# Laying out a kernel's instruction order with PSUM accesses of two engines in sequence, measured prices, a preference for long-ready TensorE groups, and shared buffers

## The chip, the cores and the metric

The kernel runs on one core of one Trainium2 chip. Time is the device time of one execution in microseconds (us). TensorE is PE in the profile, its weight loads PEld, VectorE DVE, ScalarE ACT, GpSimd POOL, SyncE SP.

## The reference

Sliding-window attention (window 64) feeds a feed-forward block whose activation is a rational function:

```python
def _attn_ref(q, k, v):                 # 8 x 8 heads x 576 x 64
    scores = scale * np.matmul(q, k.transpose(0, 1, 3, 2))
    rel = pos[:, None] - pos[None, :]
    scores = np.where((rel >= 0) & (rel < 64), scores, -1000000000.0)
    attn = np.exp(scores - np.max(scores, axis=-1, keepdims=True))
    attn = attn / (np.sum(attn, axis=-1, keepdims=True) + 1e-09)
    return np.matmul(attn, v)

def _moe_ref(x, w_in, w_out, a, b):     # x: 4608 x 512, w_in: 512 x 2048, w_out: 2048 x 512
    h = x @ w_in
    P = a[0] + a[1] * h + a[2] * h * h + a[3] * h * h * h
    Q = 1.0 + np.abs(b[0]) * np.abs(h) + np.abs(b[1]) * h * h
    return (P / (Q + 1e-06)) @ w_out
```

x is the attention's output with its heads side by side. All inputs are float32.

## The kernel before, in words

The 4608 tokens are cut into 12 chunks of 384 (`CH`). The width of 2048 is cut into 16 slices of 128. One step is one chunk with one slice: 192 steps. The phases run chunk 0 and then chunk 1 over the first eight slices, chunk 1 and then chunk 0 over the last eight, and then chunks 2 to 11 over all sixteen.

**A step.** `ffn1` makes h (128 slice rows x 384 tokens) in one of two PSUM banks (`h_ring`). Each float32 factor is held as a high and a low part, and three of the four products are taken, so h takes 12 matmuls (4 pieces of 128 x 3 terms) and the second layer 9 (3 blocks of 128 tokens x 3 terms). The gate follows: ACT reads h three times (Square into u, Abs into r, Identity into num), DVE makes Q from u and r, ACT takes Ln and Exp of it (1/Q), DVE makes P in num with two more reads of h, then the high part gh, two operations on u and the low part gl. `ffn2`, three steps later (`LAG`), multiplies gl and gh with the weights into the PSUM banks `ps_o` (o).

**An attention unit** is one chunk with one pair of heads, 48 in all: q, k and v are loaded, the scores go to `ps_s` (`score_products`), the mask is added on PE in chunks 0 to 2 and on DVE later, DVE takes the maximum, ACT makes six exponentials with sums (`unit_soft`), DVE normalises (`unit_norm`; "sm<-sm,rs"), PE transposes six blocks into `ps_s` (`unit_transpose`), ACT copies them to pT, PE multiplies by v into `ps_x` (`value_products`), and ACT and DVE split the result into xh and xl. A unit of chunk c runs beside the steps of the chunk before.

**Weights.** The 32 weight tiles (16 of w_in, 16 of w_out) are fetched into six spare places and three slots (`w_ring`, w_st), rebuilt by ACT and DVE into c (w_c) and split into high (ACT) and low (DVE) parts (`load_weight`). The next fetch of a slot is recorded behind the tile that it frees.

**The order.** Nothing is issued where it is written. A `Planner` records every operation with the engine, the bytes that it reads and writes and a price (`cost`: the time for which it occupies the engine, and the time to its result). `plan` then lays the operations out engine by engine: the one with the earliest possible start goes next, and among those ready on that engine the one recorded first. `emit` issues them in the order of the planned starts, and each engine then works through its instructions in that order, waiting where the framework's semaphores say so. All recorded instructions carry line 226, so the profile is read by tiles. `group` makes several matmuls one entry of the plan; `fill` puts warm-up matmuls in early gaps.

**Buffers.** r, u and num have two places each (`tmp`), gh and gl four each, sm and q/k two each, pT one, c two.

Of the kernel before, what the change touches and what calls it, by code (L numbers as in the profile page):

```python
# [9 lines left out]
F32 = mybir.dt.float32  # L10
# [11 lines left out]
CH = 384  # L22
# [3 lines left out]
LAG = 3  # L26
GB = 4
SLOTS = 3
WARM = 7
FILL = 430  # L30
C1AT = 0, 0, 1, 3
ON_PE = 2
# [18 lines left out]
class Planner:  # L51
# [4 lines left out]

    def __init__(self, nc, free, shares):
        self.nc, self.shares = nc, shares
        self.ops, self.group_op = [], None
        self.free = dict(free)  # L60
# [49 lines left out]
    def cost(self, engine, method, out, reads, kw, args):  # L110
        if isinstance(out, Late):
            n = out.size // 4
        else:
            n = 1
            for _, k in out.ap[1:]:
                n *= k
        if engine == "SP":
            parts = 128 if isinstance(out, Late) else (out.ap[0][1] if out.tensor.__class__.__name__ != "DRamTensorHandle" else 0)
            size = mybir.dt.size(out.dtype) * n * (parts or out.ap[0][1])
            return 400, 400, size  # L120
        if engine == "PE":
            if method == "transpose":
                return 109, 270, 0
            if isinstance(args[2], Late):
                n = args[2].size // 4
            else:
                n = 1
                for _, k in args[2].ap[1:]:
                    n *= k
                if args[2].dtype == F32:  # L130
                    return (45, 270, 0) if args[1].ap[0][1] == 64 else (52, 225, 0)
            return n * 0.452, n * 0.452 + 165, 0
        if engine == "ACT":
            if "accum_out" in kw:
                return 343, 450, 0
            f = args[2] if len(args) > 2 else None
            occ = 58 + 0.813 * n
            if n == 512:
                occ = 640 if method == "copy" and getattr(out, "dtype", None) == F16 else 510
            for k in ("scale", "bias"):  # L140
                if isinstance(kw.get(k), bass.AP):
                    occ += 92
            if f in (AF.Ln, AF.Exp):
                occ += 55
            return occ, occ + 120, 0
        if engine == "DVE":
            if method == "tensor_reduce":
                n = 1
                for _, k in reads[0].ap[1:]:
                    n *= k  # L150
            if n < 16:
                return 90, 185, 0
            occ = 65 + 1.045 * n
            if isinstance(kw.get("scalar"), bass.AP):
                occ += 62
            return occ, occ + 85, 0
        if engine == "POOL":
            return (n * 2.0 + 60, n * 2.0 + 100, 0) if method in ("tensor_scalar", "tensor_copy") else (n * 2.4 + 130, n * 2.4 + 170, 0)

    def add(self, op):  # L160
        op.index, op.before, op.after = len(self.ops), set(), []
        op.ready = max([self.known.get(name, 0) for name, *_ in op.reads + op.writes], default=0)
        for is_write, spans in ((False, op.reads), (True, op.writes)):
            for name, p0, p1, b0, b1 in spans:
                for q0, q1, c0, c1, other, wrote in self.hist.get(name, ()):
                    if (wrote or is_write) and p0 < q1 and q0 < p1 and b0 < c1 and c0 < b1:
                        op.before.add(other)
# [6 lines left out]
        for wrote, spans in ((False, op.reads), (True, op.writes)):  # L174
            for name, p0, p1, b0, b1 in spans:
                h = self.hist.setdefault(name, [])
                if wrote:
                    h[:] = [x for x in h if not (p0 <= x[0] and x[1] <= p1 and b0 <= x[2] and x[3] <= b1)]
                h.append((p0, p1, b0, b1, op.index, wrote))
                if name in self.shares:  # L180
                    self.hist.setdefault(self.shares[name], []).append((0, 128, 0, 1 << 20, op.index, False))

    def plan(self):
# [6 lines left out]
        for _ in self.ops:  # L190
            start, engine = min((max(self.free[e], min(o.ready for o in w)), e) for e, w in waiting.items() if w)
            op = min((o for o in waiting[engine] if o.ready <= start), key=lambda o: o.index)
            waiting[engine].remove(op)
# [35 lines left out]
class Recorder:  # L229
# [3 lines left out]
    def __getattr__(self, method):  # L233
        return lambda *args, **kw: self.planner.record(self.engine, self.owner, method, args, kw)


# [11 lines left out]
def swa_rational_ffn(ctx: ExitStack, tc: tile.TileContext, qk, v, w_in, w_out, out):  # L248
# [56 lines left out]

    warm = const.tile([P, 512], BF16, name="warm")
    nc.vector.memset(warm, 0.0)
    for _ in range(WARM):
        nc.tensor.matmul(ps_o[2], warm[:, 0:P], warm, start=True, stop=True)
    make_mask()  # L310
# [28 lines left out]
    UNIT = QKAB + TC * P  # L339
    qk_ring = Ring(ring, 2, [P, QKAB], F32, "qk")  # L340
    vt_ring = Ring(ring, 2, [P, TC * P], F32, "vt")
    w_ring = Ring(ring, SLOTS, [P, 1026], F32, "w_st")
    spare = [late.tile([P, H * NCC * P], F32, name=f"early_{n}", tag=f"late_{n}") for n in ("wi_h", "wi_l")]
    spare_slots = [t[:, k * 1026:(k + 1) * 1026] for k in range(H * NCC * P // 1026) for t in spare]
    c_ring = Ring(ring, 2, [P, 512], F32, "w_c")
    top_ring = Ring(const, 0, [], F32, "top")
    top_ring.tiles = tops
    sm_ring = Ring(ring, 2, [P, 2, PR, P], F32, "sm")
    pT_ring = Ring(ring, 1, [P, 2, PR * P], F32, "pT")
    small = {n: Ring(ring, 2, [P, 2 * PR], F32, n) for n in ("nmx", "sums", "rs")}  # L350
    tmp = {n: Ring(ring, 2, [P, CH], F32, n) for n in ("r", "u", "num")}
    g_ring = [Ring(ring, GB, [P, CH], F32R, n) for n in ("gh", "gl")]
    ob_ring = Ring(ring, 2, [P, DO], F32, "ob")

    shares = {t.tensor.name: f"late_{n}" for t, n in zip(early + spare, ("wo_l", "wo_h", "wi_h", "wi_l"))}
    pl = Planner(nc, dict(DVE=4700, ACT=2100, PE=WARM * 430 + 1200, POOL=5000, SP=750), shares)
    pl.ready_at(mask, 4300)
# [12 lines left out]
    def load_weight(which, i):  # L370
        w = staged.pop((which, i))
        f = (lambda t: t.rearrange("p c n -> p (c n)")) if which == "in" else (lambda t: t)
        hi_name, lo_name = ("wi_h", "wi_l") if which == "in" else ("wo_h", "wo_l")
        top, c = top_ring(), c_ring()
        low = w.bitcast(U32)[:, 0:1024].rearrange("p (n two) -> p n two", two=2)[:, :, 1]
# [13 lines left out]
    def load_qk(c, hp):  # L389
        qk_t = early[hp // 2][:, hp % 2 * UNIT:hp % 2 * UNIT + QKAB] if c == 0 else qk_ring()  # L390
        pl.sync.dma_start(out=qk_t, in_=qk[hp, c])
# [48 lines left out]
    def score_maximum(c, hp):  # L440
        u = live[c, hp]
        on_pe, ps, both, m = u["on_pe"], u["ps"], u["both"], u["m"]
        sm, nmx = u["sm"], u["nmx"] = sm_ring(), small["nmx"]().rearrange("p (z r) -> p z r", z=2)
        if not on_pe:
# [30 lines left out]
    def unit_transpose(c, hp):  # L475
        u = live[c, hp]
        ps, both = two_banks(c, hp, True)
        with pl.group():
            for j in range(2 * PR):
                pl.tensor.transpose(ps[j // PR][:, (j % PR) * P:(j % PR + 1) * P], u["sm"][:, j, :], ident)  # L480
        pT = u["pT"] = pT_ring()
        if both is not None:
# [33 lines left out]

    def ffn1(c, i):
        h = h_ring()[:, 0:CH]
        n = 0
# [9 lines left out]
        r, u, num = (tmp[n]() for n in ("r", "u", "num"))  # L529
        gh, gl = (g() for g in g_ring)  # L530
        pl.scalar.activation(u, h, AF.Square)
        pl.scalar.activation(r, h, AF.Abs, scale=b_raw[:, 0:1])
        pl.scalar.activation(num, h, AF.Identity, scale=a_sb[:, 3:4], bias=a_sb[:, 2:3])
# [9 lines left out]
        gs[c, i] = gh, gl  # L543
# [4 lines left out]
    part = {}  # L548

    def ffn2(s):  # L550
# [89 lines left out]
    for s in range(total + LAG):  # L640
# [3 lines left out]
        if s < total:  # L644
            ffn1(*steps[s])
        for fn, *args in todo.get(s, ()):
# [4 lines left out]
    pl.plan()  # L651
    pl.fill("PE", ps_o[2].tensor.name, FILL, (nc.tensor.matmul, (ps_o[2], warm[:, 0:P], warm), dict(start=True, stop=True)))
    pl.emit()
# [37 lines left out]
```

## Time and profile before

| | |
|---|---|
| median of 3 runs | 982.18 us (982.14 to 982.31) |
| the profiled execution | 982.07 us, of which the span in the profile is 980.3 |
| mean granted TensorE clock | 0.997 |
| busy: PE, DVE, ACT | 952.6 (97%), 911.2 (93%), 698.5 us (71%) |
| bytes by DMA | 68.38 MB, mean 70 GB/s |

The rows of the trace are read thus. A timeline row is start, duration, engine, line, operation and output<-inputs, then a count and, in brackets, the idle time of the engine before it and what ended that. A row of the waits is engine and output, what it waited for, total us, number of times and the longest. Bars of successive matmuls overlap, since a matmul starts before the one ahead of it has drained; the spacing of their starts is what they cost. A stage row has the window, its length, and busy time with instruction counts for PE, PEld, DVE, ACT and POOL, then the granted clock, the DMA share and GB/s.

### The profile page before, as it was taken

Reading aid. Unit: us, or ns where it says so; the run is one execution under the profiler, and the core shown is the slowest. Engines: PE = TensorE matmul, PEld = TensorE weight load, DVE = VectorE, ACT = ScalarE, POOL = GpSimd, SP = SyncE. Lnnn points to the kernel's source line nnn. Section 1 sums busy time; section 2 is a strip of 40 time slices with the busy share of each in tenths; the row PEclk is TensorE's granted clock in tenths of the full one; section 3 lists DMA queues with packets and bytes.
Section 4 is the critical chain, followed back from the end, with each engine's and each line's share of the span. In section 5 each row is a group of like instructions: output and inputs, shape, how many; then the busy total and the mean of one; then the engine's idle time right before and its main releaser. Section 6 shows DMA issues by size and latency. Waiting matters only on the chain.

```text
span 980.3 us, 17701 instructions
## 1 busy us (share of the span) xinstructions
PE 952.6 (97%) x6672; PEld 824.6 (84%) x6675; DVE 911.2 (93%) x1747; ACT 698.5 (71%) x1737; POOL 4.4 (0%) x20
## 2 busy tenths in 40 slices
PE   8899999999999999999999999999999999999998
PEld 5677788888888888888888888888888888888996
DVE  6999999998999999999999999999999899999996
ACT  7988777776667667767677677667766776676664
POOL 1000000000000000000000000000000000000000
PEclk9999999999999999999999999999999999999999
DMA  9344341313103103103102200210310310300000
GB/s 360 127 171 147 122 150 39 96 50 117 51 1 117 35 17 118 35 17 116 37 17 74 79 17 26 93 51 1 118 35 17 118 35 18 100 1 2 33 1 32
DMA packets 24564, 68.38 MB, mean 70 GB/s; under 512 B 2720, under 2 KB 2720, under 8 KB 24480
## 3 DMA queue, kind: packets, MB, share of 16 engines
q1 hardware_dynamic: 24480, 67.27, 20.2%
q8 instruction: 52, 0.85, 0.4%
q14 instruction: 32, 0.26, 0.1%
HBM read 57.03 MB, written 10.22 MB: 69 GB/s over the span
## 4 chain that ended last, share of the span: by engine, by line
PE 64%; DVE 19%; ACT 10%; issue 2%; DMA 1%; ACTq 0%; DVEq 0%
PE o L226 29%; PE h L226 28%; DVE u L226 6%; PE ps_s L226 5%; ACT sm L226 4%; DVE num L226 3%; PE ps_x L226 3%; ACT r L226 2%; DVE gh L226 2%; DVE sm L226 2%; DVE nmx L226 1%; ACT u L226 1%; DVE gl L226 1%; DMA w_st<-w_out 1%; ACT num L226 1%
## 5 line engine op out<-in xcount | busy, mean ns | idle before, releaser
L226 PE MATMUL h<-xl,wi_h 128*128 128x384 f32 x768 | 260.4, 339 | 7.7 <-DVE num L226 6.2
L226 PE MATMUL h<-xh,wi_l 128*128 128x384 f32 x768 | 258.1, 336 | 0.0
L226 PE MATMUL h<-xh,wi_h 128*128 128x384 f32 x768 | 257.9, 336 | 0.0
L226 PE MATMUL o<-wo_h,gl 128*128 128x512 f32 x576 | 236.5, 411 | 2.5 <-DVE gl L226 1.7
L226 PE MATMUL o<-wo_h,gh 128*128 128x512 f32 x576 | 228.2, 396 | 0.0
L226 PE MATMUL o<-wo_l,gh 128*128 128x512 f32 x576 | 227.0, 394 | 0.0
L226 ACT ACTIVATE u<-h 128x384 f32<-128x384 f32 x192 | 94.2, 491 | 158.4 <-PE h L226 153.6
L226 PEld LDWEIGHTS h<-xl,wi_h 128*128 128x128 f32 x768 | 144.2, 188 | 20.3 <-DVE num L226 10.2
L226 PEld LDWEIGHTS h<-xh,wi_h 128*128 128x128 f32 x768 | 144.2, 188 | 7.2
L226 ACT ACTIVATE num<-h,ab_sb 128x384 f32<-128x384 f32 x192 | 129.7, 675 | 25.7 <-PE h L226 15.6
L226 PEld LDWEIGHTS h<-xh,wi_l 128*128 128x128 f32 x768 | 144.2, 188 | 0.3 <-DVE wi_l L226 0.3
L226 ACT ACTIVATE r<-u 128x384 f32<-128x384 f32 x192 | 101.3, 527 | 48.1 <-DVE u L226 44.8
L226 PEld LDWEIGHTS o<-wo_h,gl 128*128 128x128 f32 x576 | 108.1, 188 | 29.0 <-issue 5.1
L226 PEld LDWEIGHTS o<-wo_h,gh 128*128 128x128 f32 x576 | 108.5, 188 | 26.3
L226 DVE SCALAR_TENSOR_TENSOR gh<-num,ab_sb,r 128x384 fp32r<-128x384 f32 x192 | 117.9, 614 | 8.7 <-ACT r L226 1.6
L226 PEld LDWEIGHTS o<-wo_l,gh 128*128 128x128 f32 x576 | 108.7, 189 | 16.5
L226 DVE SCALAR_TENSOR_TENSOR num<-num,ab_sb,h 128x384 f32<-128x384 f32 x192 | 117.3, 611 | 5.6 <-ACT r L226 1.5
L226 DVE SCALAR_TENSOR_TENSOR u<-u,b_sb,r 128x384 f32<-128x384 f32 x192 | 117.9, 614 | 2.9 <-ACT r L226 1.0
L226 DVE SCALAR_TENSOR_TENSOR u<-num,ab_sb,u 128x384 f32<-128x384 f32 x192 | 118.1, 615 | 2.7
L226 ACT ACTIVATE r<-h,ab_sb 128x384 f32<-128x384 f32 x192 | 111.4, 580 | 11.1 <-DVE num L226 11.1
L226 DVE SCALAR_TENSOR_TENSOR u<-u,gh 128x384 f32<-128x384 f32 x192 | 106.4, 554 | 2.7
L226 DVE TENSOR_TENSOR num<-num,h 128x384 f32<-128x384 f32 x192 | 105.0, 549 | 3.5 <-ACT r L226 2.2
(74 smaller groups left out, 983.6 us busy)
## 6 DMA issues: line engine op xcount, KB each, us to landing
qk<-qk SPq DMA_DIRECT2D x44, 419.0 KB, 4.2
vt<-v SPq DMA_DIRECT2D x44, 384.0 KB, 3.6
out<-ob SPq DMA_DIRECT2D x33, 256.0 KB, 2.1
w_st<-w_out SPq DMA_DIRECT2D x15, 512.0 KB, 3.5
w_st<-w_in SPq DMA_DIRECT2D x11, 512.0 KB, 3.6
early<-qk SPq DMA_DIRECT2D x4, 419.0 KB, 5.5
early<-v SPq DMA_DIRECT2D x4, 384.0 KB, 8.1
early_wi_l<-w_in SPq DMA_DIRECT2D x3, 512.0 KB, 9.4
```

The source lines that it names most:

```text
L226: call(*[value(x) for x in args], **{k: value(x) for k, x in kw.items()})
```

## The change

What it does:

- PSUM: for the PSUM tensors (`banks`) the planner makes two accesses by different engines depend on each other in the order recorded, even where both only read.
- Prices: a matmul column 0.4545 ns instead of 0.452; an exponential with a sum 386 ns when it reads SBUF (343 from PSUM, as before); a 512-wide ACT copy from PSUM 466; 50 ns more for a block of transposes.
- TensorE takes, in the plan, the first-recorded group among those that have been ready for at least 300 ns (`MARGIN`), and any ready group only where there is none.
- Gate: r, u and num are taken from one set of 12 places (`Slots`), three for each gate; the two DVE operations on num that read h are recorded ahead of the one on u. The code can join two steps in one gate, but with `ALONE = 188, 4` none of the 192 steps is joined.
- Buffers: c is written over the first half of the slot that it is made from; pT over sm; q/k has one place, with room of their own for the first two units of chunk 1; sm has room of its own for the last two units of chunk 0. The warm-up operand is 128 columns read four times.

```diff
+PAIRS = 2, 2
+TMP = 6
+ALONE = 188, 4
+MARGIN = dict(PE=300)
...
-            return n * 0.452, n * 0.452 + 165, 0
+            return n * 0.4545, n * 0.4545 + 165, 0
...
-                return 343, 450, 0
+                return (343, 450, 0) if reads[0].tensor.name in self.banks else (386, 490, 0)
...
+                if reads[0].tensor.name in self.banks:
+                    occ = 466
...
-                    if (wrote or is_write) and p0 < q1 and q0 < p1 and b0 < c1 and c0 < b1:
+                    apart = self.ops[other].engine != op.engine
+                    if name in self.banks and apart or (wrote or is_write) and p0 < q1 and q0 < p1 and b0 < c1 and c0 < b1:
...
-                if wrote:
+                if wrote and name not in self.banks:
...
-            op = min((o for o in waiting[engine] if o.ready <= start), key=lambda o: o.index)
+            able = [o for o in waiting[engine] if o.ready <= start]
+            op = min([o for o in able if o.ready <= start - MARGIN.get(engine, 0)] or able, key=lambda o: o.index)
...
+class Slots:
+    def __init__(self, pool, n, shape, dtype, name):
+        self.tiles = [pool.tile([shape[0], 2, *shape[1:]], dtype, name=f"{name}_{k}") for k in range(n)]
+        self.n = 0
+
+    def __call__(self, size):
+        t, k = self.tiles[self.n // 2 % len(self.tiles)], self.n % 2
+        self.n += size
+        return t if size == 2 else t[:, k]
...
-    warm = const.tile([P, 512], BF16, name="warm")
+    warm = const.tile([P, P], BF16, name="warm")
+    warm_up = (ps_o[2], warm, warm.unsqueeze(1).broadcast_to([P, 4, P]))
...
-    qk_ring = Ring(ring, 2, [P, QKAB], F32, "qk")
+    qk_ring = Ring(ring, 1, [P, QKAB], F32, "qk")
...
-    pT_ring = Ring(ring, 1, [P, 2, PR * P], F32, "pT")
-    tmp = {n: Ring(ring, 2, [P, CH], F32, n) for n in ("r", "u", "num")}
-    g_ring = [Ring(ring, GB, [P, CH], F32R, n) for n in ("gh", "gl")]
+    tmp = Slots(ring, TMP, [P, CH], F32, "tmp")
+    g_ring = [Slots(ring, n, [P, CH], F32R, name) for n, name in zip(PAIRS, ("gh", "gl"))]
...
-        top, c = top_ring(), c_ring()
+        top, c = top_ring(), w[:, 0:512]
...
+        elif c == 1 and hp < 2:
+            qk_t = early[hp][:, 2 * UNIT:2 * UNIT + QKAB]
...
+        if c == 0 and hp >= 2:
+            sm = spare[hp - 2][:, SPARES * 1026:SPARES * 1026 + 2 * PR * P].rearrange("p (z r c) -> p z r c", z=2, c=P)
...
-        with pl.group():
+        with pl.group(50):
...
-        pT = u["pT"] = pT_ring()
+        pT = u["pT"] = u["sm"].rearrange("p (z r) c -> p z (r c)", z=2)
...
+    def gate(group, hs):
+        size = len(group)
+        num, u, r = (tmp(size) for _ in range(3))
+        gh, gl = (g(size) for g in g_ring)
+        for k, h in enumerate(hs):
+            u1, r1, num1 = (t if size == 1 else t[:, k] for t in (u, r, num))
+            pl.scalar.activation(u1, h, AF.Square)
+            pl.scalar.activation(r1, h, AF.Abs, scale=b_raw[:, 0:1])
+            pl.scalar.activation(num1, h, AF.Identity, scale=a_sb[:, 3:4], bias=a_sb[:, 2:3])
+            pl.vector.tensor_tensor(out=num1, in0=num1, in1=h, op=ALU.mult)
+            pl.vector.scalar_tensor_tensor(out=num1, in0=num1, scalar=a_sb[:, 1:2], in1=h, op0=ALU.add, op1=ALU.mult)
         pl.vector.scalar_tensor_tensor(out=u, in0=u, scalar=b_sb[:, 1:2], in1=r, op0=ALU.mult, op1=ALU.add)
         pl.scalar.activation(r, u, AF.Ln, bias=QADD)
         pl.scalar.activation(r, r, AF.Exp, scale=-1.0)
-        pl.vector.tensor_tensor(out=num, in0=num, in1=h, op=ALU.mult)
-        pl.vector.scalar_tensor_tensor(out=num, in0=num, scalar=a_sb[:, 1:2], in1=h, op0=ALU.add, op1=ALU.mult)
...
+    groups = [[s] for s in range(ALONE[0])] + [[s, s + 1] for s in range(ALONE[0], total - ALONE[1], 2)]
+    groups += [[s] for s in range(total - ALONE[1], total)]
```

More of the change, by code (lines that the diff above doesn't have):

```diff
@@ L26 @@
 LAG = 3
-GB = 4
+PAIRS = 2, 2
+TMP = 6
+ALONE = 188, 4
 SLOTS = 3
@@ L55, with __init__ @@
     DMA_LANES = 8
-    def __init__(self, nc, free, shares):
+    def __init__(self, nc, free, shares, banks):
         self.nc, self.shares = nc, shares
         self.ops, self.group_op = [], None
-        self.free = dict(free)
+        self.free, self.banks = dict(free), set(banks)
         self.hist, self.known, self.loads = {}, {}, []
@@ L304, in swa_rational_ffn @@
     b_sb = const.tile([P, 2], F32, name="b_sb")
-    warm = const.tile([P, 512], BF16, name="warm")
+    warm = const.tile([P, P], BF16, name="warm")
     nc.vector.memset(warm, 0.0)
+    warm_up = (ps_o[2], warm, warm.unsqueeze(1).broadcast_to([P, 4, P]))
     for _ in range(WARM):
-        nc.tensor.matmul(ps_o[2], warm[:, 0:P], warm, start=True, stop=True)
+        nc.tensor.matmul(*warm_up, start=True, stop=True)
     make_mask()
@@ L343, in swa_rational_ffn @@
     spare = [late.tile([P, H * NCC * P], F32, name=f"early_{n}", tag=f"late_{n}") for n in ("wi_h", "wi_l")]
-    spare_slots = [t[:, k * 1026:(k + 1) * 1026] for k in range(H * NCC * P // 1026) for t in spare]
-    c_ring = Ring(ring, 2, [P, 512], F32, "w_c")
+    SPARES = H * NCC * P // 1026
+    spare_slots = [t[:, k * 1026:(k + 1) * 1026] for k in range(SPARES) for t in spare]
     top_ring = Ring(const, 0, [], F32, "top")
@@ L348, in swa_rational_ffn @@
     sm_ring = Ring(ring, 2, [P, 2, PR, P], F32, "sm")
-    pT_ring = Ring(ring, 1, [P, 2, PR * P], F32, "pT")
     small = {n: Ring(ring, 2, [P, 2 * PR], F32, n) for n in ("nmx", "sums", "rs")}
-    tmp = {n: Ring(ring, 2, [P, CH], F32, n) for n in ("r", "u", "num")}
-    g_ring = [Ring(ring, GB, [P, CH], F32R, n) for n in ("gh", "gl")]
+    tmp = Slots(ring, TMP, [P, CH], F32, "tmp")
+    g_ring = [Slots(ring, n, [P, CH], F32R, name) for n, name in zip(PAIRS, ("gh", "gl"))]
     ob_ring = Ring(ring, 2, [P, DO], F32, "ob")
     shares = {t.tensor.name: f"late_{n}" for t, n in zip(early + spare, ("wo_l", "wo_h", "wi_h", "wi_l"))}
-    pl = Planner(nc, dict(DVE=4700, ACT=2100, PE=WARM * 430 + 1200, POOL=5000, SP=750), shares)
+    pl = Planner(nc, dict(DVE=4700, ACT=2100, PE=WARM * 430 + 1200, POOL=5000, SP=750), shares, [t.tensor.name for t in [ps_s, ps_x, *ps_o, *h_ring.tiles]])
     pl.ready_at(mask, 4300)
@@ L389, in load_qk @@
     def load_qk(c, hp):
-        qk_t = early[hp // 2][:, hp % 2 * UNIT:hp % 2 * UNIT + QKAB] if c == 0 else qk_ring()
+        if c == 0:
+            qk_t = early[hp // 2][:, hp % 2 * UNIT:hp % 2 * UNIT + QKAB]
+        elif c == 1 and hp < 2:
+            qk_t = early[hp][:, 2 * UNIT:2 * UNIT + QKAB]
+        else:
+            qk_t = qk_ring()
         pl.sync.dma_start(out=qk_t, in_=qk[hp, c])
@@ L442, in score_maximum @@
         on_pe, ps, both, m = u["on_pe"], u["ps"], u["both"], u["m"]
-        sm, nmx = u["sm"], u["nmx"] = sm_ring(), small["nmx"]().rearrange("p (z r) -> p z r", z=2)
+        if c == 0 and hp >= 2:
+            sm = spare[hp - 2][:, SPARES * 1026:SPARES * 1026 + 2 * PR * P].rearrange("p (z r c) -> p z r c", z=2, c=P)
+        else:
+            sm = sm_ring()
+        nmx = small["nmx"]().rearrange("p (z r) -> p z r", z=2)
+        u["sm"], u["nmx"] = sm, nmx
         if not on_pe:
@@ L515, in swa_rational_ffn, with ffn1 @@
     gs = {}
-    def ffn1(c, i):
-        h = h_ring()[:, 0:CH]
+    def ffn1(c, i, h):
         n = 0
@@ L528, in ffn1 @@
                         n += 1
[L529 to L533, printed above, removed]
+    def gate(group, hs):
[9 more added lines that the diff above has]
+            pl.vector.scalar_tensor_tensor(out=num1, in0=num1, scalar=a_sb[:, 1:2], in1=h, op0=ALU.add, op1=ALU.mult)
         pl.vector.scalar_tensor_tensor(out=u, in0=u, scalar=b_sb[:, 1:2], in1=r, op0=ALU.mult, op1=ALU.add)
@@ L542, in ffn1 @@
         pl.vector.tensor_tensor(out=gl, in0=u, in1=r, op=ALU.mult)
-        gs[c, i] = gh, gl
+        for k, s in enumerate(group):
+            gs[steps[s]] = (gh, gl) if size == 1 else (gh[:, k], gl[:, k])
     phases = [(0, 0, H), (1, 0, H), (1, H, NF), (0, H, NF)] + [(c, 0, NF) for c in range(2, NCH)]
@@ L548, in swa_rational_ffn @@
     part = {}
+    groups = [[s] for s in range(ALONE[0])] + [[s, s + 1] for s in range(ALONE[0], total - ALONE[1], 2)]
+    groups += [[s] for s in range(total - ALONE[1], total)]
+    group_of = {s: g for g in groups for s in g}
     def ffn2(s):
@@ L644, in swa_rational_ffn @@
         if s < total:
-            ffn1(*steps[s])
+            group = group_of[s]
+            if s == group[0]:
+                hs = [h_ring()[:, 0:CH] for _ in group]
+            ffn1(*steps[s], hs[s - group[0]])
+            if s == group[-1]:
+                gate(group, hs)
         for fn, *args in todo.get(s, ()):
@@ L651, in swa_rational_ffn @@
     pl.plan()
-    pl.fill("PE", ps_o[2].tensor.name, FILL, (nc.tensor.matmul, (ps_o[2], warm[:, 0:P], warm), dict(start=True, stop=True)))
+    pl.fill("PE", ps_o[2].tensor.name, FILL, (nc.tensor.matmul, warm_up, dict(start=True, stop=True)))
     pl.emit()
```

## The prediction

> **What bounds the kernel now.** I read the page's busy line and chain first, then busy time by stage, then what TensorE waited for in each stage, and last the timeline round one repeated wait.
>
> ```profile
> span 980.3 us, 17701 instructions
> PE 952.6 (97%) x6672; PEld 824.6 (84%) x6675; DVE 911.2 (93%) x1747; ACT 698.5 (71%) x1737; POOL 4.4 (0%) x20
> ...
> PE 64%; DVE 19%; ACT 10%; issue 2%; DMA 1%; ACTq 0%; DVEq 0%
> ```
>
> TensorE (PE) is bound over most of the span, but 29% of the chain that ended last runs through VectorE (DVE) and ScalarE (ACT). A mean hides where, so the stages come next: window, then PE, PEld, DVE and ACT busy.
>
> ```profile
> 0.00:25.00 25.00, 21.19 (x230) 13.63 (x233) 16.55 (x39) 17.73 (x67) 4.38 (x20) 0.93 0.94 361
> 25.00:150.00 125.00, 112.78 (x747) 92.82 (x746) 124.24 (x241) 106.24 (x243) 0.00 (x0) 1.00 0.41 139
> 150.00:300.00 150.00, 146.08 (x1099) 126.33 (x1099) 139.97 (x273) 107.38 (x284) 0.00 (x0) 1.00 0.19 63
> 300.00:900.00 600.00, 596.79 (x4229) 524.59 (x4228) 561.18 (x1074) 420.99 (x1057) 0.00 (x0) 1.00 0.16 52
> ```
>
> There are two regimes. From 25 to 150 us, while the 32 weight tiles are split into a high and a low half, DVE is busy for 124.24 of 125 us and PE idles for 12.2: DVE is the bound. From 150 us on PE is the bound and DVE has slack. The waits of PE in the two regimes, the second list from 150 us to the end:
>
> ```profile
> PE h L226 <- DVE num L226: 6.2, 8, 1.4
> PE ps_x L226 <- ACT pT L226: 2.1, 3, 0.9
> PE o L226 <- DVE gl L226: 1.7, 3, 0.9
> ...
> PE ps_s L226 <- DVE sm L226: 3.1, 6, 1.0
> PE ps_s L226 <- ACT ob L226: 2.7, 4, 0.7
> PE o L226 <- DVE ob L226: 0.5, 1, 0.5
> PE ps_x L226 <- ACT pT L226: 0.2, 1, 0.2
> PE ps_s L226 <- ACT pT L226: 0.2, 1, 0.2
> ```
>
> After 150 us nearly all that is left is one kind of stop: the six transposes of an attention unit (ps_s), which PE meets in its queue before the normalised scores (sm) are there. Here is one, from the timelines of PE, ACT and DVE:
>
> ```profile
> 450.59 0.33 PE L226 MATMUL h<-xh,wi_h 128*128 128x384 f32 x1
> 450.76 0.34 PE L226 MATMUL h<-xh,wi_l 128*128 128x384 f32 x1
> 451.77 0.85 PE L226 MATMUL ps_s<-ident,sm 128*128 128x128 f32 x6 [0.68 <-ACT ob L226]
> 452.38 0.48 PE L226 MATMUL o<-wo_h,gl 128*128 128x512 f32 x1
> ...
> 447.79 0.40 ACT L226 ACTIVATE sm<-sm,nmx 128x128 f32<-128x128 f32 x1
> 448.18 0.39 ACT L226 ACTIVATE sm<-sm,nmx 128x128 f32<-128x128 f32 x1
> ...
> 448.48 0.55 DVE L226 TENSOR_TENSOR gl<-u,r 128x384 fp32r<-128x384 f32 x1
> 450.24 0.17 DVE L226 TENSOR_SCALAR sums<-sums 128x6 f32<-128x6 f32 x1 [1.21 <-ACT sm L226]
> 450.44 0.19 DVE L226 RECIPROCAL rs<-sums 128x6 f32<-128x6 f32 x1
> 450.67 0.96 DVE L226 TENSOR_TENSOR sm<-sm,rs 128x768 f32<-128x768 f32 x1
> ```
>
> The last six exponentials start 0.39 us apart (447.79, 448.18); DVE waits 1.21 us for them, sm ends at 451.63 and the transposes start at 451.77. The release is printed as "ACT ob", but sm is what ended 0.14 us earlier. It is one of the eleven ps_s stops in the list above.
>
> **The change, part by part.** The same matmuls, ACT and DVE instructions and DMAs are issued, in equal number (but for warm-up matmuls that fill early gaps); what changes is their order and the buffers that they use.
>
> *Prices.* The old planner charged 343 ns for each exponential with a sum. In the start-up, with scores read from PSUM, that is right; from chunk 3 on they come from SBUF.
>
> ```profile
> 8.43 0.35 ACT L226 ACTIVATE sm<-ps_s,nmx 128x128 f32<-128x128 f32 x1
> 8.78 0.36 ACT L226 ACTIVATE sm<-ps_s,nmx 128x128 f32<-128x128 f32 x1
> ```
>
> 0.35 us here against 0.39 above: per unit the old plan believes the sums 5 x 0.043 + 0.04 (end of the last: 450 against 490) = 0.26 us too early. The new one charges 386 there. An order written by a plan that is 0.26 us early puts the transposes exactly where PE finds them late. The other prices (0.4545 for 0.452 ns a column, 466 for a 512-wide PSUM copy, 50 ns more for a block of transposes) move the plan by less per item, and cost nothing on the chip.
>
> *TensorE takes groups ready for 300 ns.* This makes the order robust against what price error is left: unless nothing else is available, the transposes are put behind a block of work that is surely ready. Such work exists: the o matmul at 452.38 uses a gl that was finished by 449.03 (448.48 + 0.55) or earlier, 2.7 us before the stop. What is late next is the copy of the transposes and the value products; the tile view of sm says how much time they have:
>
> ```profile
> L226 PE MATMUL ps_s<-ident,sm x240: 270/273/303, 153.8 to 882.8; 128*128 128x128 f32 x120
> ```
>
> Forty units in 729 us are 18.7 us apart, and one block of PE work put in front is 2.0 us (12 h matmuls 0.17 us apart), so moving them by one block is covered. Worth: from 150 us on the idle listed is 3.1 + 2.7 + 0.5 + 0.2 + 0.2 = 6.7 us in 13 stops. The true loss is larger, because the bar of a matmul (0.34) overlaps the next by 0.17 (450.59 to 450.76): 451.77 - 450.76 - 0.17 = 0.84 lost where 0.68 is shown, 0.16 more each, so 6.7 + 13 x 0.16 = 8.8 us. Bounds: 0 if every stop reappears elsewhere; 13.4 if the other 29 of the 40 units also lose up to the 0.16 that a bar can hide (4.6). I take 8.8, the listed stops.
>
> *Two engines' accesses to one PSUM tensor in sequence.* The program that runs already keeps them apart; only the plan did not know.
>
> ```profile
> ACT r L226 <- DVE num L226: 11.1, 20, 0.7
> ...
> 321.67 0.58 ACT L226 ACTIVATE r<-h,ab_sb 128x384 f32<-128x384 f32 x1 [0.62 <-DVE num L226]
> ...
> 321.08 0.56 DVE L226 TENSOR_TENSOR num<-num,h 128x384 f32<-128x384 f32 x1
> ```
>
> ACT's read of h waits until DVE's read of the same h ends (321.64), though neither writes it. These 11.1 us go, since the plan now puts all three ACT reads ahead of DVE's. ACT is busy 421 of 600 us, so I cost that at nothing. The Trainium skill, page "PSUM — Partial Sum Buffer", section "PSUM bank collisions raise a hardware error", says that any two engines touching one bank in the same quadrant must be kept in sequence, reads against reads included; by that rule this edit can take no wait out of the program and only place it, and this row agrees with it.
>
> *Buffers shared, and the gate's order.* r, u and num come from 12 slots, so four gates can be open instead of two, and the two DVE operations that free h are listed first. In the DVE-bound stage ACT waits for exactly these buffers:
>
> ```profile
> ACT num L226 <- DVE u L226: 8.7, 7, 1.6
> ACT u L226 <- DVE gl L226: 2.8, 9, 0.8
> ```
>
> That wait stands in front of DVE's num, which frees h, for which PE idles 6.2 us. With it gone PE can be further ahead when the DVE-bound stage ends, but DVE's 124.24 us of work stay: total time falls only by the extra lead, at most two h blocks (4.0 us), and could rise by one (2.0) if DVE's newer num work holds up gl. I take one block, 2.0, since the h wait is the largest of the three in this stage. The two num operations ahead of u lengthen a gate by about 1 us; the gl above lies over 3 us ahead of its use.
>
> *Weight slot reused in place.* c is written over the slot it is made from, so the next fetch waits for the last subtract instead of the combine:
>
> ```profile
> 128.37 3.98 SPq L226 DMA_DIRECT2D w_st<-w_out  x2
> ...
> 132.52 0.78 ACT L226 CAST top<-w_st 128x512 f16<-128x512 bf16 x1
> ...
> 127.60 0.69 DVE L226 SCALAR_TENSOR_TENSOR w_c<-w_st,top 128x512 uint32<-128x512 uint32 x1
> 129.73 0.69 DVE L226 TENSOR_TENSOR wo_l<-w_c,wo_h 128x512 fp32r<-128x512 f32 x1
> ...
> 140.71 0.69 DVE L226 SCALAR_TENSOR_TENSOR w_c<-w_st,top 128x512 uint32<-128x512 uint32 x1
> ...
> w_st<-w_out SPq DMA_DIRECT2D x15, 512.0 KB, 3.5
> w_st<-w_in SPq DMA_DIRECT2D x11, 512.0 KB, 3.6
> ```
>
> The fetch issued at 128.37, right behind the combine's end (128.29), would now wait until 130.42: 2.1 us. The fetched tile's top cast ends at 133.30 and its combine starts at 140.71, so 7.4 us of DVE backlog cover it: nothing. Behind the waiting fetch on SP stand q, k and v loads of the next units, 18.7 us apart.
>
> *q/k ring of one, transposes written back into sm, four-times-repeated warm operand.* A sm slot is held until its value products, but is next written two units, 37 us, later; one q/k buffer is refilled once its scores are done, a unit ahead. The first two units of chunk 1 and the last two of chunk 0 get room of their own, which takes waits away from the first 75 us. The warm operand is as many columns. Nothing; the 3.8 us that PE idles in the first 25 bound it to both sides, and I keep 1 us of them.
>
> Sum: the profiled execution took 982.07 us (span 980.3 and 1.8 outside), 0.11 under the median. 982.07 - 8.8 - 2.0 = 971.3, so 971.
>
> **Rivals.** *The lead is worth more.* If four open gates fed PE through the whole 25 to 150 us, most of its 12.2 us would come back on top of the 8.8: about 963. For it: the 6.2 us behind num. Against it: DVE has 0.76 us free there.
>
> *The stops only move.* The plan may be no truer than the old one elsewhere, and transposes put a block later may hold up other units. Then 982 stays, within 2 us. Against it: the late exponentials are one price that can be read off two rows. A page would see it otherwise: the Trainium skill, "Perfetto Trace Analysis", section "Identifying the Most-Contended Engine", says to judge TensorE by weight loads, not matmul busy time; by 84% there would be 156 us to win. The 0.17 us spacing of h matmuls with their loads hidden says that what reordering can win is the idle time, not that.
>
> *Slower: the weight fetch becomes the bound.* If DVE's order now runs a combine within 2.1 us of its top cast, the 7.4 us cover is gone and each fetch adds its 2.1 us; with 15 + 11 - 3 = 23 refetches over three slots that is 23 x 2.1 / 3 = 16 us, and with the gain of 10.8 still there 987. Against it: DVE stays full, so its backlog stays.
>
> **How the numbers follow.** Faster by the forecast's mechanism, 966 to 977: 0.53. More lead, below 966: 0.13. Stops only move, 977 to 984: 0.17, of which 0.07 is still faster by more than 0.2% (about 2 us, what a measurement here can tell from no change). Weight fetch or another new wait, above 984: 0.17. So faster 0.73, same 0.10, slower 0.17. Cutting a tenth on each side leaves 963 to 985; the likeliest case alone is 966 to 977.
>
> **What would show it.** Right: after 150 us the list of PE's waits loses ps_s behind sm and ob, and "ACT r behind DVE num" is gone; DVE stays full from 25 to 150 us while PE idles some 10 us there. Wrong: PE waits for o behind gl or ps_x behind pT after 150 us; a DVE that is idle before 150 us behind ACT top with ACT behind a weight DMA; or a PE that gains nearly all of the 12.2 us before 150.

## The result, and the profile after

The changed kernel takes 975.26 us (median of 6 runs, 973.75 to 976.19), the kernel before 982.16 on the same chip (980.44 to 983.67). The ratio is 0.9929, with a 95% interval of 0.9916 to 0.9942: faster by 7 us, inside the predicted 963 to 985, but 4 us short of the 971 that was forecast. The profiled execution took 975.82 us, with a span of 974.0, against 982.07 and 980.3.

The page's busy line and the shares of its chain, after:

```profile
span 974.0 us, 17551 instructions
PE 948.9 (97%) x6673; PEld 828.6 (85%) x6673; DVE 903.2 (93%) x1747; ACT 692.8 (71%) x1737; POOL 4.4 (0%) x20
...
PE 83%; DVE 12%; ACT 2%; DMA 1%; issue 1%; SPq 0%; ACTq 0%; DVEq 0%
```

The chain now runs through PE for 83% instead of 64%. The three stages from 25 us on, in the columns used before (window, length, PE, PEld, DVE, ACT busy):

```profile
25.00:150.00 125.00, 113.59 (x746) 94.73 (x742) 124.20 (x240) 105.78 (x238) 0.00 (x0) 0.99 0.41 136
150.00:300.00 150.00, 145.82 (x1102) 127.49 (x1102) 137.25 (x274) 106.43 (x290) 0.00 (x0) 1.00 0.21 69
300.00:900.00 600.00, 599.33 (x4256) 531.68 (x4255) 562.54 (x1085) 420.89 (x1065) 0.00 (x0) 1.00 0.15 51
```

The DVE-bound stage is as it was, with DVE busy for 124.20 of 125 us. From 300 to 900 us PE gained 2.5 us of busy time (596.79 to 599.33). Between 150 and 300 it gained nothing (146.08 to 145.82), and that is the first sign that something new is wrong there. What PE waited for from 150 us to the end:

```profile
PE ps_s L233 <- DVE sm L233: 2.1, 1, 2.1
PE h L233 <- DVE tmp L233: 1.1, 2, 0.6
PE ps_x L233 <- ACT sm L233: 0.9, 1, 0.9
PE ps_s L233 <- ACT ob L233: 0.7, 1, 0.7
PE o L233 <- DVE gl L233: 0.2, 1, 0.2
```

The eleven stops at transposes are two, but one of the two is 2.1 us long, longer than any in the list of before (1.0). A unit where the stop is gone, from the timelines of DVE and PE:

```profile
430.53 0.96 DVE L233 TENSOR_TENSOR sm<-sm,rs 128x768 f32<-128x768 f32 x1
...
431.96 0.39 PE L233 MATMUL o<-wo_h,gh 128*128 128x512 f32 x1
432.19 0.82 PE L233 MATMUL ps_s<-ident,sm 128*128 128x128 f32 x6
```

sm is finished at 431.49 and the transposes start at 432.19, right behind an o matmul: now sm waits for PE.

The bars hide part of a stop, so for all 40 units after 150 us I took the start of the transposes less the start of the matmul ahead, less about 0.17 us behind an h matmul or 0.23 behind an o matmul (the usual distance, as 431.96 to 432.19). That loss sums to some 9.7 us before and 3.0 after.

One thing must be put right ahead of the experiments. The condition with which the changed planner picks the price of an exponential, `reads[0].tensor.name in self.banks`, looks at the first thing read by name, and that is the bias nmx, which never lies in PSUM. So the new plan charges 386 ns (450 becomes 490) for every exponential with a sum, those of the start-up that read PSUM too. My text of the change had these at 343.

### The profile page after: what moved, and what is told of

It reads as the page before. It is cut to its first block, busy times and chain, and to the rows that moved or that the text cites. A ratio compares the mean times of both kernels' runs of the same rounds, so it can differ in the third digit from the quotient of the medians.

```text
span 974.0 us, 17551 instructions
## 1 busy us (share of the span) xinstructions
PE 948.9 (97%) x6673; PEld 828.6 (85%) x6673; DVE 903.2 (93%) x1747; ACT 692.8 (71%) x1737; POOL 4.4 (0%) x20
## 4 chain that ended last, share of the span: by engine, by line
PE 83%; DVE 12%; ACT 2%; DMA 1%; issue 1%; SPq 0%; ACTq 0%; DVEq 0%
PE o L233 38%; PE h L233 36%; PE ps_s L233 6%; DVE tmp L233 5%; PE ps_x L233 4%; DVE w_st L233 1%; DVE gh L233 1%; DVE gl L233 1%; DVE wo_l L233 1%; DVE wi_l L233 1%; ACT tmp L233 1%; DMA early_wi_h<-w_in 1%; DVE nmx L233 1%; DVE sm L233 1%; ACT sm L233 1%
## 5 line engine op out<-in xcount | busy, mean ns | idle before, releaser
L233 ACT ACTIVATE tmp<-h 128x384 f32<-128x384 f32 x192 | 94.6, 493 | 205.6 <-PE h L233 205.3
L233 ACT ACTIVATE tmp<-tmp 128x384 f32<-128x384 f32 x384 | 201.9, 528 | 40.4 <-DVE tmp L233 35.6
L233 ACT ACTIVATE tmp<-h,ab_sb 128x384 f32<-128x384 f32 x384 | 224.5, 630 | 0.0
L233 DVE SCALAR_TENSOR_TENSOR gh<-tmp,ab_sb,tmp 128x384 fp32r<-128x384 f32 x192 | 117.5, 613 | 7.4 <-ACT tmp L233 1.2
L233 DVE SCALAR_TENSOR_TENSOR tmp<-tmp,ab_sb,h 128x384 f32<-128x384 f32 x192 | 116.8, 609 | 2.3
L233 DVE SCALAR_TENSOR_TENSOR tmp<-tmp,gh 128x384 f32<-128x384 f32 x192 | 106.0, 552 | 2.2
L233 DVE TENSOR_TENSOR tmp<-tmp,h 128x384 f32<-128x384 f32 x192 | 104.9, 546 | 0.0
L233 ACT ACTIVATE sm<-sm,nmx 128x128 f32<-128x128 f32 x216 | 83.7, 398 | 5.1 <-DVE nmx L233 5.1
L233 DVE SCALAR_TENSOR_TENSOR tmp<-tmp,b_sb,tmp 128x384 f32<-128x384 f32 x96 | 58.6, 611 | 2.3 <-ACT tmp L233 2.2
L233 DVE SCALAR_TENSOR_TENSOR tmp<-tmp,ab_sb 128x384 f32<-128x384 f32 x96 | 59.0, 615 | 1.8
```

Source lines behind the costliest of these rows:

```text
L233: call(*[value(x) for x in args], **{k: value(x) for k, x in kw.items()})
```

## The experiments

Two theories stood at the start. The price theory: the true price of the exponentials puts the transposes where sm is ready, and the 300 ns add little. The margin theory: the 300 ns do the work whatever the price. Below, "before" always means the kernel before on the same chip.

**The price alone, a first try.** In the kernel before:

```diff
-                return 343, 450, 0
+                return (386, 490, 0) if reads[0].tensor.name.startswith("sm") else (343, 450, 0)
```

> The kernel before with one price put right: an exponential with a sum that reads SBUF counts 386 ns and 490 to its end, nothing else. Price theory: the repeated stops at the transposes come from a plan that is 0.26 us early; listed ps_s waits of PE after 150 us fall from 5.8 us to under 2 and the time to 976 to 977. Margin theory (the preference for long-ready groups is what removes them): 980 to 982, ps_s waits over 4 us. Buffers theory (deeper r, u, num and the bank order): 982, ps_s waits unchanged.

981.57 against 981.50, ratio 1.0001 (0.9992 to 1.0010). The miss is my edit's: it has the same fault as the condition above, never charges 386, and gives the old program instruction for instruction. It serves as a repeat of the kernel before, and shows how well two equal programs agree: to 0.1%.

**The margin alone.** In the kernel before:

```diff
-            op = min((o for o in waiting[engine] if o.ready <= start), key=lambda o: o.index)
+            able = [o for o in waiting[engine] if o.ready <= start]
+            op = min([o for o in able if o.ready <= start - MARGIN.get(engine, 0)] or able, key=lambda o: o.index)
```

> The kernel before with TensorE in the plan preferring groups ready for 300 ns, nothing else; all prices stay. Price theory: 300 ns of margin is about the size of the 0.26 us error, so it hides a part: 977 to 980. Margin theory: 975 to 977, ps_s waits after 150 us under 2 us. Buffers theory: 982.

977.96, ratio 0.9969 (0.9956 to 0.9982). Its waits of PE from 150 us on:

```profile
PE ps_s L228 <- ACT ob L228: 2.7, 4, 0.7
...
PE ps_s L228 <- DVE sm L228: 0.3, 1, 0.3
```

Of the stops at transposes the group of four that ends "ACT ob" stays, and 3.1 us in six go to 0.3 in one. So the margin clears about half. Why 0.30 us of margin leaves the other half, when the price is only 0.26 us early, is open; the stop shown in the prediction lost 0.84 us, more than either. The run meant to have both edits has the void condition too and is the same program; it measured 978.13, ratio 0.9967 (0.9953 to 0.9981). So price and margin together, without the new buffers, were not measured.

> The kernel before with the exponential's price and the 300 ns preference, nothing else. Price and margin theories both: 974.5 to 976, the whole measured gain of 6.9 us without any of the buffers, the bank order or the gate order. Buffers theory: 980 to 982.

**The price alone, now in force**, in the kernel before:

```diff
-                return 343, 450, 0
+                return 386, 490, 0
```

> The kernel before with every exponential with a sum at 386 and 490 ns in the plan, as the changed kernel in fact charges (its condition looks at the bias, which is never in PSUM), nothing else. Price theory: the ps_s stops of PE after 150 us fall from 5.8 us to under 2 and the time by 4 to 6 us, to 976 to 978. Context theory (the price only pays with the 300 ns preference or the deeper buffers beside it): 980 to 982.

977.86, ratio 0.9958 (0.9941 to 0.9975): one price in the plan is worth 4.1 us. Waits of PE from 150 us on:

```profile
PE ps_s L226 <- DVE sm L226: 1.2, 4, 0.5
PE h L226 <- DVE num L226: 0.9, 1, 0.9
PE o L226 <- DVE ob L226: 0.8, 1, 0.8
PE ps_s L226 <- ACT pT L226: 0.2, 1, 0.2
```

The "ACT ob" group is gone. The loss at transposes, by the sum above, is 9.7 us before, 6.3 with the margin and 3.8 with the price. By this sum the price does more than the margin; the times (0.9958 and 0.9969, with intervals that overlap) don't tell the two apart.

**The changed kernel without the price** (343 and 450 for all):

> The changed kernel with the exponential's price put back to 343 ns everywhere, all else kept. Price theory: the stops come back, 980 to 982. Margin theory: the 300 ns cover the 0.26 us error, 975 to 976.5. Buffers theory: 975 to 976.5.

980.53, ratio 0.9993 (0.9983 to 1.0002): nearly the whole gain is gone, though the margin and the 12 slots are there. Its first wait from 150 us on says why:

```profile
PE ps_s L233 <- ACT ob L233: 5.2, 7, 0.9
```

The late transposes are back. In the changed kernel the price theory holds, and the margin is no substitute for it; in the kernel before, the margin alone did have a ratio of 0.9969.

**The price by where the scores lie** (`reads[0]` becomes `args[1]`, so that the scores read from PSUM cost 343 again):

> The changed kernel with 343 ns for exponentials that really read PSUM (chunks 0 to 2), as its text means, and 386 for the others. Price theory: only the order of the first 190 us can change; PE's loss in 25 to 150 us is set by DVE, so 974 to 976, within 1.5 us of the changed kernel. If prices matter there too: 972 or less.

976.01, ratio 0.9941 (0.9926 to 0.9955), the interval overlapping the changed kernel's. The fault in the condition costs nothing that can be measured: it touches the first units alone.

**The changed kernel without the margin** (`MARGIN = dict()`):

> The changed kernel without the 300 ns preference. Price theory: with right prices it is nearly idle, 975 to 977; its short stops of 0.1 to 0.3 us behind sm come back, so ps_s loss after 300 us rises from 0.8 to 2 to 4 us. Margin theory: 978 to 980.

971.59, ratio 0.9895 (0.9880 to 0.9909). Both theories missed: the margin does not help here, it costs some 3 us by the ratios (0.9929 to 0.9895). From 150 us on, a single wait is left on the list, and the stage in which the changed kernel gained nothing has 3.1 us more of PE busy time than before (149.21 against 146.08):

```profile
PE ps_s L233 <- ACT ob L233: 0.8, 1, 0.8
...
150.00:300.00 150.00, 149.21 (x1140) 130.26 (x1138) 142.94 (x280) 108.72 (x287) 0.00 (x0) 1.00 0.22 71
300.00:900.00 600.00, 600.00 (x4245) 531.95 (x4242) 562.46 (x1085) 421.29 (x1066) 0.00 (x0) 1.00 0.15 50
```

How is time lost by a rule that only takes ready work first? The transposes and score products of chunk 2's attention units (ps_s), which run beside the last eight steps of chunk 0, two steps to a unit, first of the changed kernel, then without the margin (start and length; a row is a block of six transposes or 24 products):

```profile
168.06 0.82 PE L233 MATMUL ps_s<-ident,sm 128*128 128x128 f32 x6
...
174.29 0.89 PE L233 MATMUL ps_s<-qk 64*64 64x128 f32 x24
183.60 0.82 PE L233 MATMUL ps_s<-ident,sm 128*128 128x128 f32 x6
```

```profile
166.84 0.82 PE L233 MATMUL ps_s<-ident,sm 128*128 128x128 f32 x6
...
170.97 0.89 PE L233 MATMUL ps_s<-qk 64*64 64x128 f32 x24
178.17 0.82 PE L233 MATMUL ps_s<-ident,sm 128*128 128x128 f32 x6
```

From the transposes to the next unit's products it is 6.23 us with the margin and 4.13 without, from these to the next transposes 9.31 and 7.20. Both links are 2.1 us longer, and so is the next one; the other three links between the transposes of chunk 2's first unit (154.5 us) and of its last (197.0) are as long as without the margin. In each of the three longer links PE does one block more: 12 h matmuls 0.17 us apart (2.0 us) in the first and the third, nine o matmuls 0.23 apart (2.1 us) in the second. The units follow each other, each link waiting for the one before, so these delays add up. Chunk 2's first h matmul, which needs them all, comes at 202.60 with the margin, at 195.51 without, and came at 198.32 before. This is what the margin does to this plan, and not to every plan: put into the kernel before, it leaves that matmul at 197.92.

**Where the 2.1 us stop comes from.** It stands at 209 us of the changed kernel; timelines of PE, DVE and SP's queue:

```profile
206.59 0.34 PE L233 MATMUL h<-xh,wi_l 128*128 128x384 f32 x1
208.99 0.85 PE L233 MATMUL ps_s<-ident,sm 128*128 128x128 f32 x6 [2.06 <-DVE sm L233]
...
206.69 0.69 DVE L233 TENSOR_TENSOR ob<-o,ob 128x512 f32<-128x512 f32 x1 [1.04 <-DMA ob<-part]
207.30 0.18 DVE L233 RECIPROCAL rs<-sums 128x6 f32<-128x6 f32 x1
207.89 0.95 DVE L233 TENSOR_TENSOR sm<-sm,rs 128x768 f32<-128x768 f32 x1
...
200.53 0.33 SPq L233 DMA_DIRECT2D qk<-qk  x1
...
201.60 0.42 SPq L233 DMA_DIRECT2D ob<-part  x1
```

The transposes are next in PE's order. The normalisation they wait for stands on DVE behind an addition that waits 1.04 us for the partial sums read back from memory, and that read stands on SP behind a q/k load, which must wait until the one q/k place is free. Before, the same kind of read was issued at 195.79, and DVE did not wait for it. Reading the partial sums back into a free weight slot instead of ob takes one possible reason for a late read away:

```diff
-            ob = w_ring()[:, 0:DO] if ends else ob_ring()
+            ob = w_ring()[:, 0:DO] if ends or c in part and not spill else ob_ring()
```

> The changed kernel with the three read-backs of chunk 0's partial sums going into weight slots that are free by then, so that their DMAs need not wait behind a q/k load that waits for the single q/k place. TensorE's order is the same. Queue theory: the 2.1 us stop of PE at 209 us comes from DVE waiting 1.0 us for the late read-back with the normalisation queued behind it; it shrinks by 1 to 2 us and the time falls by 1 to 3, to 972.5 to 974.5. If the stop is due to late exponentials like the others: no change, 975.

```profile
205.68 0.69 DVE L233 TENSOR_TENSOR w_st<-o,w_st 128x512 f32<-128x512 f32 x1
206.88 0.95 DVE L233 TENSOR_TENSOR sm<-sm,rs 128x768 f32<-128x768 f32 x1
...
207.98 0.85 PE L233 MATMUL ps_s<-ident,sm 128*128 128x128 f32 x6 [1.04 <-ACT tmp L233]
```

DVE's wait is gone and the stop shrinks from 2.06 to 1.04 us: half of it was this read. But the edit did not mend what it was meant to. The read still goes out behind the q/k load, at 201.43 instead of 201.60; it landed in 4.2 us instead of 5.0, and that was enough. That the q/k place makes the read late is therefore read off the queue and not shown by a run. The time, 976.41, ratio 0.9941 (0.9926 to 0.9956), does not tell 1 us from none; the span is 973.2 against 974.0. The other half of the stop stays with DVE's sums, which start at 205.48 in both kernels, behind exponentials that are late themselves.

**The margin only where units are far apart.** If the margin hurts in the dense stretch and is harmless elsewhere, this gives the whole gain back:

```diff
-            op = min([o for o in able if o.ready <= start - MARGIN.get(engine, 0)] or able, key=lambda o: o.index)
+            op = min([o for o in able if o.ready <= start - (MARGIN.get(engine, 0) if start > 215000 else 0)] or able, key=lambda o: o.index)
```

> The changed kernel with the 300 ns preference only in the part of the plan that starts after 215 us. Dense-unit theory: the preference costs its 4 us only while units follow each other every two steps (150 to 210 us), where each postponed block of transposes delays the next unit and at last the first step of chunk 2; then this kernel is as fast as without the preference, 970.5 to 972.5, with no ps_s stop of 2 us at 209 us. If the preference costs something everywhere (longer chains, more switches of PE): 973 to 976.

971.10, ratio 0.9903 (0.9888 to 0.9918), chunk 2's first h matmul at 195.81. The loss lies before 215 us of the plan; behind it the margin is worth nothing either way. Its list of PE waits from 150 us on is the one line of the kernel without a margin.

**Half the slots** (no margin, `TMP = 3`: six places, as many as r, u and num had before):

> The changed kernel without the preference and with 6 places instead of 12 for r, u and num, so two gates open as before. Depth theory (the third and fourth gate are what is worth some 6 us beside the price): 976 to 979. If the gate's order or the other buffers are it: 971 to 973.

976.23, ratio 0.9952 (0.9936 to 0.9969), against 0.9895 with twelve. That is, within the intervals, the ratio of the price alone in the kernel before (0.9958), so that beside price, places and margin the rest of the change (rings, warm operand, weight slot, sequence, other prices) is worth, on balance, no more than the 2 us or so that these runs can't tell from nothing. ACT's instructions on the places between 150 and 900 us, with the idle time ahead of them and what ended it, then what PE waited for from 150 us on, then PE's busy time from 300 to 900 us, all with six places:

```profile
L233 ACT ACTIVATE tmp<-h,ab_sb 128x384 f32<-128x384 f32 x307 | 188.0, 624 | 98.8 <-DVE tmp L233 66.2 <-PE h L233 32.5
...
L233 ACT ACTIVATE tmp<-h 128x384 f32<-128x384 f32 x154 | 75.3, 489 | 70.0 <-PE h L233 54.4 <-DVE gl L233 15.2
...
PE ps_x L233 <- ACT sm L233: 1.6, 5, 0.9
PE h L233 <- DVE tmp L233: 1.5, 2, 1.1
PE o L233 <- DVE gl L233: 1.4, 1, 1.4
PE ps_s L233 <- DVE sm L233: 0.6, 1, 0.6
...
300.00:900.00 600.00, 599.25 (x4257) 531.40 (x4256) 552.14 (x1087) 419.39 (x1066) 0.00 (x0) 1.00 0.15 50
```

And ACT's with twelve:

```profile
L233 ACT ACTIVATE tmp<-h,ab_sb 128x384 f32<-128x384 f32 x308 | 179.4, 628 | 0.0
L233 ACT ACTIVATE tmp<-tmp 128x384 f32<-128x384 f32 x312 | 164.6, 528 | 28.1 <-DVE tmp L233 23.9
```

With six places ACT's reads of h stand 66.2 + 15.2 us for places that DVE has still to free; with twelve they stand for none (the 23.9 us left there are the Ln waiting for DVE's Q). PE's list is 5.1 us in nine stops against 0.8 in one. That the one makes the other, because behind ACT's waiting instruction stand the copies and exponentials that PE needs, is an argument; and few of ACT's waits reach PE, which between 300 and 900 us is busy for 599.25 of the 600 us with six places and for 600.00 with twelve. By the first h matmuls of the chunks, the kernel with six places is 2.5 us behind at chunk 2 (197.99 against 195.51), 3.8 at chunk 3, 4.4 at chunk 11 and 6.1 at the end: the places are worth most ahead of chunk 3 and in the last chunk. The Trainium skill, "Perfetto Trace Analysis", section "Optimization Strategy", says that one gap repeating on an engine that should be saturated can mean too little room for the next tile. More room did shorten PE's list here, from 5.1 us to 0.8, though its nine stops are of four kinds and not one gap repeating.

**The gate's old order** (no margin, twelve places, num's two operations recorded after the exponential again):

> The changed kernel without the preference and with the gate recorded in the old order (DVE's operation on u ahead of the two on num that free h). Depth theory: no difference beyond 1.5 us, 970.5 to 973. If the earlier release of h is it: 975 to 978, with more waits of PE for h behind DVE.

973.13, ratio 0.9921 (0.9906 to 0.9936), just outside the 970.5 to 973 of the depth theory. The intervals of 0.9921 and 0.9895 touch, so the order is worth somewhere between nothing and 5 us, with 2.6 in the middle; the depth does more.

**No margin and the price by place:**

> The changed kernel without the preference and with 343 ns for exponentials that really read PSUM. Price theory: only the first 190 us can differ from the kernel without the preference, 970 to 973; faster than both kernels compared here in any case.

972.10, ratio 0.9911 (0.9897 to 0.9926): nothing on top. Its trace shows that long links need no margin: two of the three are here as well (6.23 and 9.30 us where the changed kernel has 6.23 and 9.31), and chunk 2's first h matmul is at 200.48, against 201.27 with the margin and the same prices.

The two best are the kernel without a margin (0.9895) and the one with a late margin (0.9903). Both beat the changed kernel's 0.9929 by some 3 us through the ratios, though the interval of the second just touches the changed kernel's; the spans of the profiled executions lie 5 us apart (968.8 and 968.9 against 974.0).

In the table, the last two columns are read off the profiled executions by counting h matmuls, 12 to a step: when chunk 2's first one starts, and how long it is from chunk 3's first to chunk 11's first. The first try of the price, the same program as the kernel before, has 197.3 and 623.9 there, so 1 us in the first and 0.3 in the second say nothing.

| kernel | price | margin | places | ratio | chunk 2 starts | chunks 3 to 10 take |
|---|---|---|---|---|---|---|
| before | 343 | none | 6 | 1 | 198.3 | 624.2 |
| before with margin | 343 | 300 | 6 | 0.9969 | 197.9 | 622.8 |
| before with price | 386 | none | 6 | 0.9958 | 200.5 | 621.9 |
| changed, six places, no margin | 386 | none | 6 | 0.9952 | 198.0 | 618.6 |
| changed, no price | 343 | 300 | 12 | 0.9993 | 200.7 | 624.3 |
| changed | 386 | 300 | 12 | 0.9929 | 202.6 | 618.4 |
| changed, late margin | 386 | 300 after 215 us | 12 | 0.9903 | 195.8 | 617.9 |
| changed, no margin | 386 | none | 12 | 0.9895 | 195.5 | 618.0 |

In the long even stretch the price is what counts: without it the changed kernel takes 624.3 us, as before, and with it 618.4. With that price, places and margin move it by under 1 us. They act ahead of chunk 3, where chunk 2's start differs by up to 7 us, and the places also in the last chunk. The step from 621.9 (the price in the kernel before) to 618.6 (six places, no margin) belongs to another part of the change, which no run separates.

## Why the prediction was right or wrong

**Two regimes: right.** In all fourteen traces DVE is busy for 123.7 to 124.9 of the 125 us between 25 and 150 us.

**Transposes found ready, 8.8 us: right in mechanism, near in size.** The loss at the transposes fell from 9.7 to 3.0 us, 6.7. Some 1 us more came from the transposes themselves. Group of these instructions from 150 us on, before and after (total, mean ns, idle ahead of it):

```profile
L226 PE MATMUL ps_s<-ident,sm 128*128 128x128 f32 x240 | 33.6, 276 | 6.0 <-DVE sm L226 3.1 <-ACT ob L226 2.7
...
L233 PE MATMUL ps_s<-ident,sm 128*128 128x128 f32 x240 | 32.7, 273 | 2.7 <-DVE sm L233 2.1 <-ACT ob L233 0.7
```

I added 0.16 us of hidden loss to the 13 listed stops and kept the other 29 units for the upper bound only. That was too low a base: in 32 of the 40 units the transposes started within 0.16 us of sm's end, and 13 of the 29 units without a listed stop lost some 0.15 us each, 1.9 us together. The listed idle ahead of transposes fell by only 3.3 us (6.0 to 2.7); as much again had been hidden under bars.

**The price as the cause: right. The margin as a robust addition: wrong, and this is the step that failed.** I wrote that "Forty units in 729 us are 18.7 us apart", so that moving a group by one block is covered. That mean hid the stretch where it is not so: chunk 2's transposes stand, in the kernel before, at 153.81, 166.39, 178.87 and 192.30, 12 to 13 us apart, in a chain where each waits for the last and chunk 2 waits for all. There a block is not free, and three links pay 2.1 us each. The rival "the stops only move" was true in this one stretch: a stop of 2.06 us at 209 where none was.

**PSUM accesses in sequence: worth nothing, as forecast, but not for the reason given.** The 11.1 us that ACT waited behind DVE's read of h are gone: from 150 to 900 us no read of h by ACT waits for DVE. But with that edit taken out of the changed kernel, the order of instructions is the same on every engine, so there was no program of its own to run, and the twelve places or the gate's new order took these waits away. This is also why the rule of the Trainium skill's "PSUM — Partial Sum Buffer", section "PSUM bank collisions raise a hardware error", changes no number here: no run shows what two engines in one bank would do.

**Buffers and the gate's order, a lead of 2.0 us: wrong place, and mis-sized.** In the DVE-bound stage, 25 to 150 us, ACT's waits for these places did go, from 8.7 + 2.8 us to nothing, but PE's wait for h, from which I took the 2.0, did not: 7.8 us in six stops, against 6.2 in eight. So the waits for places were not what held up h.

```profile
PE h L233 <- DVE tmp L233: 7.8, 6, 1.9
...
L233 ACT ACTIVATE tmp<-h,ab_sb 128x384 f32<-128x384 f32 x48 | 28.5, 640 | 0.0
```

The places are worth more, 0.9952 to 0.9895 or 5.6 us without the margin, but behind that stage, where I had put nothing on them: with six places and with twelve the transposes at 153 us stand within 0.3 us of each other, and the 2.5 us at chunk 2 come after that. ACT's slack of 421 busy in 600 us is a good reason for the long even stretch, where the places are worth 0.6 us, and none for the dense stretch and for the last chunk. In the changed kernel the margin took much of this gain away, so that it is luck in part that a sum with two wrong terms came within 4 us.

**Weight slot in place: right.** The fetch now goes behind the last subtract, and the tile is wanted 10 us later:

```profile
130.61 0.68 DVE L233 TENSOR_TENSOR wo_l<-w_st,wo_h 128x512 fp32r<-128x512 f32 x1
...
131.32 4.11 SPq L233 DMA_DIRECT2D w_st<-w_out  x2
...
136.50 0.79 ACT L233 CAST top<-w_st 128x512 f16<-128x512 bf16 x1
...
141.71 0.67 DVE L233 SCALAR_TENSOR_TENSOR w_st<-w_st,top 128x512 uint32<-128x512 uint32 x1
```

Cast at 137.29, combine at 141.71: 4.4 us of backlog left of the 7.4, and the rival of a weight-bound stage does not occur.

**One q/k place: nearly right.** It was costed at nothing; in one spot the read behind it on SP came late enough to cost DVE 1.04 us. I had named who stands behind the weight fetch on SP, but not who stands behind the q/k load. A ring of two beside twelve places does not fit, and was not tried.

**A sign of being wrong, in small.** I had named PE waiting for o behind gl, or for ps_x behind the copied transposes. The first is there with 0.2 us and the second, now that the copy lies over sm, with 0.9, each in one stop.

**The rule on weight loads.** The Trainium skill, "Perfetto Trace Analysis", section "Identifying the Most-Contended Engine", would leave PE headroom, with PEld at 85%. Against it stands the kernel without a margin: between 300 and 900 us its PE is busy for 600.00 of 600 us with PEld at 531.95, and no stop is left on the list there. A busy bar shows only that reordering these matmuls has nothing more to win; whether the matmuls themselves could be cheaper no run here shows.

Left open: price with margin in the old buffers; how much of the 2.6 us of the gate's order is real; which other part of the change takes 621.9 to 618.6 us in chunks 3 to 10; and how a price that is 0.26 us early makes stops of 0.84 us.

## What to carry to other kernels

When an order is written from a plan, read the plan's prices off the trace first: one price 43 ns too low, six times in a row, cost 4 us in the kernel before and 6 in the changed one, where a safety margin did not replace it. A margin that prefers long-ready work can delay a chain in which each link waits for the last, so look for the stretch where the chain is dense, with its own rows and not a mean over the kernel. The waits of an engine with slack are a poor count of what more places would be worth: here most of them cost the bound engine next to nothing in the even stretch, and the gain came in the dense one and at the end. Measure along the bound engine, from one fixed instruction to the next.

## What was not expected of the hardware

The first o matmul behind a block of transposes is slower than the others. In the rows below, of the kernel without a margin, the second starts 0.32 us after the first, and the third 0.24 after the second:

```profile
167.41 0.48 PE L233 MATMUL o<-wo_h,gl 128*128 128x512 f32 x1
167.73 0.39 PE L233 MATMUL o<-wo_l,gh 128*128 128x512 f32 x1
167.97 0.39 PE L233 MATMUL o<-wo_h,gh 128*128 128x512 f32 x1
```

After 150 us, 39 of the 40 blocks of transposes in this kernel are followed by such a switch, always 0.32 us long, so by an estimate it is 39 x 0.08 = 3 us that no order won back. Its cause was not tried.
